# A decode-attention kernel rewritten with semaphores by hand: 8 heads per 8 MB tile, three slots, products in place

## The chip, the cores and the metric

The kernel runs on one core of a Trainium2 chip; the other cores are idle. The metric is device time in microseconds (us), the median of several executions. A profiled execution shows a span about 2 us shorter than its timed one; the span runs from the first to the last instruction.

## The reference, cut to what matters

One token for each of four sequences goes through a layer norm, attention over a cache of 4096 keys and values with 32 heads of 128, and a small MLP.

```python
B, Sq, D = 4, 1, 640
H, Sk, Dh, F = 32, 4096, 128, 1728
q = (layernorm(x) @ wq)                        # wq: 640 x 4096
scores = einsum("bhqd,bhkd->bhqk", q, k_cache) * Dh**-0.5
o = einsum("bhqk,bhkd->bhqd", softmax(scores), v_cache)
h = x + o @ wo                                 # wo: 4096 x 640
a = layernorm(h) @ w1 + b1                     # w1: 640 x 1728
out = h + (a * tanh(softplus(a))) @ w2         # w2: 1728 x 640
```

The two caches are bf16 and hold 134 MB each. With the weights, 283.3 MB have to be read once. Each byte of K is used in one multiply and one add, so this is a kernel that moves data.

## The kernel before

K and V come in tiles of 4 heads of one sequence, 4 MB each, into four rotating slots. All loads are issued from one queue (SP), each as soon as its slot is free. VectorE (DVE) multiplies a quarter of K by the broadcast query into a `prod` buffer; TensorE (PE) folds the 128 products of a key to 16 by eight matmuls against an identity; DVE sums these 16; ScalarE (ACT) takes the exponential. PE then multiplies the weights `e` with V.

```python
def emit_mult(i, s):
    t = work.tile([P, RS, Dh], BF16, tag="prod", name="prod", bufs=2)
    nc.vector.tensor_tensor(out=t, in0=kt[i][:, s*RS:(s+1)*RS, :], in1=q_bc[...], op=ALU.mult)
def emit_fold(i, s):
    for c in range(Dh // CW):
        nc.tensor.matmul(red, lhsT=ident, rhs=t[:, :, c*CW:(c+1)*CW], start=(c == 0), stop=...)
# ... (cut)
# order of the last loads:
loads.append((load_cache, vt, A_v_cache, NT - 1, "v", 4))   # the last V, in quarters
loads.append((load_wo_late,))                               # the second half of wo
for k in reversed(range(WLATE)):                            # the first half of wo, earlier
    loads.insert(2 * ((k + 1) * N - 1), (load_wo, k))
loads.append((load_mlp,))                                   # w1 in three loads, w2 in three
```

After the last V the rest has to be done in order: O, its product with `wo`, a layer norm, `w1`, the activation, `w2`, the stores. This stretch is called the tail below.

The softmax here doesn't subtract the row's maximum and nothing guards it: scores larger than these inputs give would overflow.

## Time and profile before

| | before |
|---|---|
| time, median (three executions; 669.59 with a fourth, in the result below) | 669.33 us |
| span of the profiled run | 667.5 us |
| bytes read | 283.4 MB |
| PE / DVE busy | 64% / 62% |
| DMA, 60 to 630 us | 432 GB/s, busy share 1.00 |

The page's totals by engine:

```profile
span 667.5 us, 6967 instructions
PE 426.0 (64%) x2937; PEld 198.2 (30%) x2937; DVE 411.7 (62%) x477; ACT 75.5 (11%) x312; POOL 1.9 (0%) x9
```

The windows view of the same run, for the start, the long middle and the end. Each row gives the stretch, its length, the busy time of each engine with its instructions, then the granted PE clock, the busy share of the DMA engines, and the GB/s moved. A DMA packet (one row of a load) counts in the stretch in which it starts:

```profile
core 0: us, PE busy (x) PEld busy (x) DVE busy (x) ACT busy (x) POOL busy (x), PEclk, DMA share, GB/s
0.00:60.00 60.00, 34.76 (x182) 14.52 (x183) 34.68 (x62) 11.79 (x30) 1.94 (x9) 0.95 0.98 411
60.00:630.00 570.00, 362.19 (x2390) 164.65 (x2389) 363.39 (x384) 57.97 (x267) 0.00 (x0) 0.83 1.00 432
630.00:667.50 37.50, 29.02 (x367) 19.05 (x365) 13.62 (x33) 5.76 (x15) 0.00 (x0) 0.68 0.81 337
```

The middle decides how to think about this kernel. No compute engine is near full, but the DMA share is 1.00 for 570 us.

The timeline view of the tail (start, duration, engine, line, operation; in brackets the idle time before it and what ended it):

```profile
646.49 0.61 PE L352 MATMUL pv_124<-v_3666,e 128*16 128x512 bf16 x8 [1.04 <-DMA v_3666<-in_A_v_cache_dram]
...
652.66 0.69 PE L409 MATMUL y_ps<-a_3986,wo_late 128*128 128x4 bf16 x20 [0.86 <-DMA wo_late<-in_A_wo_dram]
...
656.90 1.89 PE L537 MATMUL h_ps<-cen,w_slot 128*64 128x4 bf16 x28 [0.20 <-DMA w_slot<-in_B_w_dram]
...
662.41 1.91 PE L585 MATMUL y_ps<-w_sb,act 128*4 128x160 bf16 x52
664.37 0.33 DVE L591 CAST o_bf<-y_ps 128x160 bf16<-128x160 f32 x1 [2.24 <-PE y_ps L585]
664.72 0.67 SPq L594 DMA_DIRECT2D out_dram<-o_bf  x2
```

PE starts on the last quarter of V at 646.5 us, on the last part of `wo` at 652.7, on the second load of `w1` at 656.9, each time after a wait for that load.

### The profile page before, as it was taken

Reading aid. Unit: us, or ns where it says so; the run is one execution under the profiler, and the core shown is the slowest. Engines: PE = TensorE matmul, PEld = TensorE weight load, DVE = VectorE, ACT = ScalarE, POOL = GpSimd, SP = SyncE. Lnnn points to the kernel's source line nnn. Section 1 sums busy time; section 2 is a strip of 40 time slices with the busy share of each in tenths; the row PEclk is TensorE's granted clock in tenths of the full one; section 3 lists DMA queues with packets and bytes.
Section 4 is the critical chain, followed back from the end, with each engine's and each line's share of the span. In section 5 each row is a group of like instructions: output and inputs, shape, how many; then the busy total and the mean of one; then the engine's idle time right before and its main releaser. Section 6 shows DMA issues by size and latency. Waiting matters only on the chain.

```text
span 667.5 us, 6967 instructions
## 1 busy us (share of the span) xinstructions
PE 426.0 (64%) x2937; PEld 198.2 (30%) x2937; DVE 411.7 (62%) x477; ACT 75.5 (11%) x312; POOL 1.9 (0%) x9
## 2 busy tenths in 40 slices
PE   1967546694567675574764865568765657747586
PEld 0323222242223332232332422233322223323145
DVE  3387565686565676465675666557765657757542
ACT  0401001010001110011100110101100111001011
POOL 1000000000000000000000000000000000000000
PEclk9987789897788976788877788979867898778895
DMA  9999999999999999999999999999999999999995
GB/s 376 440 411 438 419 438 435 432 427 439 432 427 430 430 436 429 438 437 423 432 437 431 433 428 436 437 430 427 434 437 436 429 429 432 438 431 430 427 415 241
DMA packets 12591, 283.81 MB, mean 425 GB/s; under 512 B 1608, under 2 KB 1680, under 8 KB 3728
## 3 DMA queue, kind: packets, MB, share of 16 engines
q1 hardware_dynamic: 12224, 283.27, 98.8%
q8 instruction: 23, 0.38, 0.2%
q10 hardware_dynamic: 336, 0.10, 0.1%
q14 instruction: 8, 0.07, 0.0%
HBM read 283.36 MB, written 0.01 MB: 424 GB/s over the span
## 4 chain that ended last, share of the span: by engine, by line
DMA 61%; DVE 19%; PE 18%; issue 1%; ACT 0%; SPq 0%; DVEq 0%; ACTq 0%
DVE prod L284 16%; PE red L296 14%; DMA k_1005<-in_A_k_cache_dram 4%; DMA k_530<-in_A_k_cache_dram 4%; DMA k_1480<-in_A_k_cache_dram 4%; DMA k_1955<-in_A_k_cache_dram 4%; DMA k_2881<-in_A_k_cache_dram 4%; DMA k_2428<-in_A_k_cache_dram 4%; DMA k_3334<-in_A_k_cache_dram 4%; DMA k_1691<-in_A_k_cache_dram 4%; DMA k_310<-in_A_k_cache_dram 4%; DMA k_3092<-in_A_k_cache_dram 4%; DMA k_1216<-in_A_k_cache_dram 3%; DMA k_741<-in_A_k_cache_dram 3%; DMA v_3666<-in_A_v_cache_dram 3%; DMA k_2166<-in_A_k_cache_dram 3%
## 5 line engine op out<-in xcount | busy, mean ns | idle before, releaser
L296 PE MATMUL red<-prod,ident 128*128 128x512 bf16 x1024 | 300.1, 451 | 218.9 <-DVE prod L284 218.0
L296 PEld LDWEIGHTS <-ident 128*128 128x128 bf16 x1024 | 116.0, 114 | 385.2 <-issue 317.6
L313 DVE TENSOR_REDUCE s_f<-red 128x32 f32<-128x512 f32 x128 | 88.1, 688 | 79.4 <-PE red L296 79.2
L316 ACT ACTIVATE ex<-s_f 128x32 bf16<-128x32 f32 x128 | 29.3, 229 | 516.6 <-DVE s_f L313 516.6
L323 DVE TENSOR_TENSOR e<-ex,hmask 128x128 bf16<-128x128 bf16 x128 | 36.5, 285 | 6.1 <-ACT ex L316 6.1
L373 PEld LDWEIGHTS o_ps<-selo,pv_sb 128*128 128x128 f32 x256 | 34.0, 194 | 6.0 <-ACT pv_sb L363 1.2
L352 PEld LDWEIGHTS <-e 128*16 128x16 bf16 x1024 | 22.6, 89 | 36.8 <-issue 15.5
L373 PE MATMUL o_ps<-selo,pv_sb 128*128 128x4 f32 x256 | 31.1, 245 | 0.7 <-ACT pv_sb L363 0.7
L316 ACT ACTIVATION_READ_ACCUMULATOR ex<-s_f 128x1 f32 x128 | 23.9, 187 | 0.1
L284 DVE TENSOR_TENSOR prod<-k_79,qbc 128x4096 bf16<-128x4096 bf16 x4 | 9.1, 2287 | 17.6 <-DMA k_79<-in_A_k_cache_dram 17.6
L379 DVE TENSOR_TENSOR OT<-o_ps,rl 128x16 bf16<-128x16 f32 x8 | 1.6, 195 | 21.0 <-PE o_ps L373 21.0
L256 PE MATMUL q_ps<-wq_74,lnT 128*4 128x512 bf16 x32 | 10.7, 470 | 4.7 <-DMA wq_74<-in_A_wq_dram 4.7
L284 DVE TENSOR_TENSOR prod<-k_1691,qbc 128x4096 bf16<-128x4096 bf16 x4 | 9.1, 2286 | 5.7 <-DMA k_1691<-in_A_k_cache_dram 5.7
L284 DVE TENSOR_TENSOR prod<-k_3092,qbc 128x4096 bf16<-128x4096 bf16 x4 | 9.1, 2286 | 5.7 <-DMA k_3092<-in_A_k_cache_dram 5.7
L284 DVE TENSOR_TENSOR prod<-k_1216,qbc 128x4096 bf16<-128x4096 bf16 x4 | 9.1, 2286 | 4.9 <-DMA k_1216<-in_A_k_cache_dram 4.9
L284 DVE TENSOR_TENSOR prod<-k_3545,qbc 128x4096 bf16<-128x4096 bf16 x4 | 9.1, 2286 | 4.9 <-DMA k_3545<-in_A_k_cache_dram 4.9
L284 DVE TENSOR_TENSOR prod<-k_741,qbc 128x4096 bf16<-128x4096 bf16 x4 | 9.1, 2285 | 4.9 <-DMA k_741<-in_A_k_cache_dram 4.9
L284 DVE TENSOR_TENSOR prod<-k_903,qbc 128x4096 bf16<-128x4096 bf16 x4 | 9.1, 2287 | 4.8 <-DMA k_903<-in_A_k_cache_dram 4.8
L284 DVE TENSOR_TENSOR prod<-k_428,qbc 128x4096 bf16<-128x4096 bf16 x4 | 9.1, 2286 | 4.6 <-DMA k_428<-in_A_k_cache_dram 4.6
L284 DVE TENSOR_TENSOR prod<-k_1378,qbc 128x4096 bf16<-128x4096 bf16 x4 | 9.1, 2286 | 4.5 <-DMA k_1378<-in_A_k_cache_dram 4.5
L284 DVE TENSOR_TENSOR prod<-k_1853,qbc 128x4096 bf16<-128x4096 bf16 x4 | 9.1, 2286 | 4.5 <-DMA k_1853<-in_A_k_cache_dram 4.5
L284 DVE TENSOR_TENSOR prod<-k_530,qbc 128x4096 bf16<-128x4096 bf16 x4 | 9.1, 2285 | 4.4 <-DMA k_530<-in_A_k_cache_dram 4.4
(179 smaller groups left out, 376.2 us busy)
## 6 DMA issues: line engine op xcount, KB each, us to landing
wq_74<-in_A_wq_dram SPq DMA_DIRECT2D x1, 4096.0 KB
k_79<-in_A_k_cache_dram SPq DMA_DIRECT2D x1, 4096.0 KB, 24.8
k_81<-in_A_k_cache_dram SPq DMA_DIRECT2D x1, 4096.0 KB, 33.9
v_83<-in_A_v_cache_dram SPq DMA_DIRECT2D x1, 4096.0 KB, 17.3
k_244<-in_A_k_cache_dram SPq DMA_DIRECT2D x1, 4096.0 KB
v_246<-in_A_v_cache_dram SPq DMA_DIRECT2D x1, 4096.0 KB
k_310<-in_A_k_cache_dram SPq DMA_DIRECT2D x1, 4096.0 KB, 24.6
v_314<-in_A_v_cache_dram SPq DMA_DIRECT2D x1, 4096.0 KB, 32.1
```

Of the source, the lines that this page charges most:

```text
L256: nc.tensor.matmul(q_ps[:, :], lhsT=lnT[:, c, :], rhs=wq_t[c // WQC][:, o : o + 512], start=(c == 0), stop=(c == DC - 1),)
L284: nc.vector.tensor_tensor(out=t[:, :, :], in0=kt[i][:, s * RS : (s + 1) * RS, :], in1=q_bc[hg][:, b, :].unsqueeze(1).to_broadcast([P, RS, ...
L296: nc.tensor.matmul(red[:, :, :], lhsT=ident[:, :], rhs=t[:, :, c * CW : (c + 1) * CW], start=(c == 0), stop=(c == Dh // CW - 1),)
L313: nc.vector.tensor_reduce(out=s_t[i][:, sl], in_=reds.pop((i, s))[:, :, :], axis=AX.X, op=ALU.add)
L316: nc.scalar.activation(out=ex_t[i][:, sl], in_=s_t[i][:, sl], func=ACT.Exp, scale=SCALE, accum_out=rs_t[hg][:, b, s : s + 1],)
L323: nc.vector.tensor_tensor(out=e_t[i][:, sl, :], in0=ex_t[i][:, sl].unsqueeze(2).to_broadcast([P, RS, G]), in1=hmask[:, :].unsqueeze(1).to_ ...
L352: nc.tensor.matmul(pvs[i % 2][k * QD : k * QD + RQ * G, :], lhsT=e_t[i][:, u * RQ : (u + 1) * RQ, :], rhs=vt[i][:, u * RQ : (u + 1) * RQ, ...
L373: nc.tensor.matmul(o_ps[hg][:, b, :], lhsT=t[:, r, :], rhs=selo[:, r, :], start=(r == 0), stop=(r == RQ - 1),)
L379: nc.vector.tensor_tensor(out=OT[:, hg * G : (hg + 1) * G, :].rearrange("p g b -> p b g"), in0=o_ps.pop(hg)[:, :, :], in1=rl.pop(hg)[:, :] ...
```

## The change

The intent: fewer and larger loads, fewer instructions, no scheduling layer. The main parts are these.

- Tiles of 8 heads, 8 MB per load, in three slots of 64 KB per partition. The product overwrites K in its slot.
- 960 of the 1024 fold matmuls reuse the identity already in PE and have no weight load. PE's program is a loop.
- O is accumulated with one row per head and batch (`selo` as weights) instead of one column.
- With three such slots the program has about 16 KB per partition of SBUF left for all the rest (bytes 16512 to 32736 in its code), and `wo` needs 40 KB, so all of `wo` is loaded after the last V. The last V is one load.
- Every engine's program is written in order, with waits on counted semaphores.

```diff
-    G = 4
+    G = 8
-    NSLOT = 4
+    # three slots A, B, C of R * Dh elements
+    KS = {0: "A", 1: "B", 2: "A", 3: "B"}
+    VS = {0: "C", 1: "C", 2: "A", 3: "C"}
 # loads, one group of four tiles
+            k_load(i)                     # after PV of tile i-2
+            k_load(i + 1)                 # after the last fold of i-1
+            v_load(i)                     # after PV of i-1
+            k_load(i + 2)                 # after the last fold of i
+            v_load(i + 1)                 # after PV of i
+            k_load(i + 3)                 # after the last fold of i+1
+            v_load(i + 2)                 # after the last fold of i+2
+            v_load(i + 3)                 # after PV of i+1
 # ... and after the last tile: wo in 4 loads, w1 in 2, w2's remainder, w2 in 3
 # products in place
+                lambda: v.tensor_tensor(
+                    out=t, in0=t, in1=q_bc[:, hg, b, :].unsqueeze(1).to_broadcast([P, RS, Dh]),
 # one weight load per 16 fold matmuls
+            mm(*args, skip=False) if first else mm_same(*args)
 # O in row form
+                o_ps, selo[:, r, BG - G - b * G : 2 * BG - G - b * G], pv_sb[:, r, :],
 # ... (most of the diff is cut)
```

## The prediction

> **What bounds the kernel now.** The DMA stream. The windows view gives DMA share 1.00 and 432 GB/s over 60:630 us (431 to 433 in each 100 us). PE is busy 64%, DVE 62% (page). The chain of waits is 61% DMA; its DVE and PE pieces are work done while the next loads are queued. [...]283.3 MB at 432 GB/s is 656 us of the 667.5 us span. The rest: the first 10 us at 351 GB/s (about 2 us lost), and 10.6 us from the last w1 chunk's landing (656.9) to the end. Rearranging PE or DVE work can gain little[...].
>
> **What the change does.**
> - Same bytes. K/V come in 32 loads of 8 MB (64 KB rows) instead of 64 of 4 MB: perhaps less overhead; my estimate is 0 to 3 us.
> - PE: 1024 fold matmuls stay, 960 of their weight loads go (451 ns mean each now). 1024 PV matmuls stay (1.90 us per 32). Off the critical path.
> - DVE: same elements, half the instructions. Per 8 MB tile, estimated from 2.29 us per 4096 columns and 0.69 us per 512 reduced: 18 + 5 + 2.5 = 25.5 us, against 38.8 us of loads. Still hidden.
> - Slots: three of 8 MB, products in place, so K is held until its last fold. Landings lag the average byte count by about 5 us. At 19.4 us per load I find every slot free before its turn; the smallest slack is V of a group's third tile (waits for the fold after PV), about 6 us[...]. Few small bubbles: 0 to 4 us.
> - Start: all of q comes before the first product, so DVE starts some 10 us later, but the first V needs its slot only at 52 us: hidden.
> - Tail: worse. All of wo (5.2 MB, 160 matmuls, weights now strided) comes after the last V; before, half was done earlier. The last V lands whole, not in quarters. After it I estimate, from the trace: PV 3.9, copy and O 2, sums, `om` and transposes 3, wo 160 matmuls at 33 to 67 ns partly waiting for loads, layer norm 1.3, w1 70 at 67 ns 4.7, activation and 40 small matmuls 2.5 to 4, w2 2.2, output 3.5: 29 to 33 us. Before, 21 us from the last V quarter (646.5) to the end. The last V lands about 6 us earlier (2.6 MB more behind it). Net +2 to +6 us.
>
> **Sum.** Steady state -3 to +4, tail +2 to +6, start 0, lighter synchronisation perhaps -1 to -3. A hand-made schedule was probably tuned, so I lean low: 668 us timed, 659 to 677. Chances: faster by over 2% 0.06, within 2% 0.87, slower 0.07.
>
> **What would show each step.** Windows: 60:630 at 431 to 435 GB/s, DMA share 0.99 or more, no 10 us window under 0.9. Queue's waits: K/V issues wait for PV or fold, yet no gap. Groups: [...]960 fewer PEld, PE busy down by 40 us or more with no time gained. Timeline at the end: last V landing near 640, 27 to 33 us from there to the end, PE waiting little on DMA.
>
> **What would make it wrong.** If 8 MB loads with 64 KB row pitch run at another rate (1% is 6.5 us either way); if a slot frees late in each group, bubbles of several us times four; if PE's loop or self-loading weights cost more; if the tail overlaps better than my serial sum.

## The result

| | before | after |
|---|---|---|
| time, median | 669.59 us | 669.56 us |
| PE busy / weight loads busy | 426.0 / 198.2 us | 394.1 / 79.4 us |
| DMA, 60 to 630 us | 432 GB/s | 433 GB/s |
| PE starts on the last of V | 646.5 us | 637.2 us |
| PE starts on the last part of `wo` | 652.7 us | 650.7 us |
| last byte of the weights moved | 662.6 us | 661.4 us |
| end of span | 667.5 us | 667.4 us |

The ratio after to before is 1.000, with a 95% interval of 0.9985 to 1.0014. Ratios here are the mean time of one kernel's runs over that of the other's of the same rounds, so not quite the ratio of the medians quoted. The time of the last byte comes from the trace's packet records: each weight load has its own row size, so its packets can be told apart.

The page and the windows view of the changed kernel:

```profile
span 667.4 us, 5166 instructions
PE 394.1 (59%) x2729; PEld 79.4 (12%) x1769; DVE 406.5 (61%) x250; ACT 41.0 (6%) x157; POOL 2.6 (0%) x14
```

```profile
0.00:60.00 60.00, 32.11 (x234) 13.19 (x183) 23.86 (x23) 7.38 (x15) 2.02 (x11) 0.77 0.99 419
60.00:630.00 570.00, 339.02 (x2081) 47.45 (x1170) 377.43 (x205) 29.96 (x138) 0.61 (x3) 0.80 1.00 433
630.00:667.40 37.40, 22.97 (x416) 18.77 (x416) 5.18 (x22) 3.70 (x5) 0.00 (x0) 0.60 0.76 311
```

A quarter of the instructions and 119 us of weight loads are gone, and the middle looks the same, since the DMA share was 1.00 and still is. The tail in the timeline of the changed kernel:

```profile
637.21 5.27 PE L657 MATMUL pv<-slotC,e 128*32 128x512 bf16 x64 [11.19 <-PEq L44]
...
642.41 1.76 PE L657 MATMUL y_ps<-a_t,slotB 128*128 128x4 bf16 x40
...
650.66 1.73 PE L657 MATMUL y_ps<-a_t,slotB 128*128 128x4 bf16 x40 [1.15 <-PEq L44]
...
654.00 2.73 PE L657 MATMUL red<-cen,slotB 128*64 128x4 bf16 x42 [0.30 <-PEq L44]
...
661.44 1.96 PE L657 MATMUL red<-slotA,act 128*4 128x160 bf16 x52
663.44 0.32 DVE L653 CAST o_bf<-red 128x160 bf16<-128x160 f32 x1 [2.53 <-PE red L657]
663.79 1.33 SPq L239 DMA_DIRECT2D out_dram<-o_bf  x4
```

In this hand-synchronised program the profile names PE's own sequencer (PEq) as what ended a wait, at L44, the `wait_ge` of the program's helper; what it waited for has to be worked out from the program. The 11.19 us are the wait for the last V, the 1.15 us the wait for the last quarter of `wo`.

At the last V the changed kernel is 9.3 us ahead. About 6.2 us of that is only order, by an estimate at 433 GB/s: 2.7 MB more (half of `wo` and the remainder of w2) now lie behind V. Some 3 us are a real lead. At the last part of `wo` the lead is 2.0 us, at the last byte 1.2, at the end 0.1. So a gain was there and was given back in the last 30 us. The windows show the GB/s of one place, 650 to 655 us, first before, then after, then for the loads of the changed kernel without any compute (stream8, below):

```profile
650.00:655.00 5.00, 3.59 (x82) 3.16 (x78) 0.97 (x7) 1.38 (x2) 0.00 (x0) 0.50 1.03 423
```

```profile
650.00:655.00 5.00, 3.77 (x60) 3.62 (x61) 1.54 (x11) 0.83 (x2) 0.00 (x0) 0.50 1.03 385
```

```profile
650.00:655.00 5.00, 0.00 (x0) 0.00 (x0) 1.00 1.01 377
```

The third line warns against a hasty reading: 385 is lower than 423, but the same loads move no more when nothing runs beside them. (The windows of runs without compute have columns for DVE and POOL alone.)

The theory going into the experiments was: the stream of bytes bounds the middle, and at the end the last byte and the chain of work after the last V arrive together. The rivals were: a gain of PE or DVE that late slots eat up; 8 MB loads that run at another rate; and an end set by the chain after the last V alone.

### The profile page after: what moved, and what is told of

It reads as the page before. It is cut to its first block, busy times and chain, and to the rows that moved or that the text cites. A ratio compares the mean times of both kernels' runs of the same rounds, so it can differ in the third digit from the quotient of the medians.

```text
span 667.4 us, 5166 instructions
## 1 busy us (share of the span) xinstructions
PE 394.1 (59%) x2729; PEld 79.4 (12%) x1769; DVE 406.5 (61%) x250; ACT 41.0 (6%) x157; POOL 2.6 (0%) x14
## 5 line engine op out<-in xcount | busy, mean ns | idle before, releaser
L466 DVE TENSOR_TENSOR slotA<-slotA,q_bc 128x8192 bf16<-128x8192 bf16 x32 | 140.7, 4416 | 110.9 <-DMA slotA<-in_A_k_cache_dram 110.7
L466 DVE TENSOR_TENSOR slotB<-slotB,q_bc 128x8192 bf16<-128x8192 bf16 x32 | 140.7, 4416 | 16.3 <-DMA slotB<-in_A_k_cache_dram 16.3
L667 PE MATMUL red<-slotA,ident 128*128 128x512 bf16 x480 | 141.0, 459 | 0.0
L477 DVE TENSOR_REDUCE s_f<-red 128x64 f32<-128x1024 f32 x64 | 78.1, 1220 | 96.9 <-PE red L667 96.8
L667 PE MATMUL red<-slotB,ident 128*128 128x512 bf16 x480 | 123.3, 415 | 0.0
L657 PE MATMUL red<-slotA,ident 128*128 128x512 bf16 x32 | 14.2, 445 | 119.3 <-PEq L44 119.3
L657 PE MATMUL pv<-slotC,e 128*32 128x512 bf16 x768 | 52.4, 434 | 42.7 <-PEq L44 42.7
L657 PE MATMUL red<-slotB,ident 128*128 128x512 bf16 x32 | 14.1, 441 | 87.0 <-PEq L44 87.0
L348 ACT ACTIVATE ex<-s_f 128x64 bf16<-128x64 f32 x64 | 16.4, 256 | 502.3 <-DVE s_f L477 502.3
L491 DVE TENSOR_TENSOR e<-ex,hmask 128x512 bf16<-128x512 bf16 x64 | 39.8, 682 | 0.0
L657 PEld LDWEIGHTS pv<-slotC,e 128*32 128x32 bf16 x768 | 22.5, 108 | 103.0 <-issue 89.4
L657 PE MATMUL o_ps<-pv_sb,selo 128*32 128x128 f32 x128 | 17.0, 276 | 0.0
## 6 DMA issues: line engine op xcount, KB each, us to landing
slotA<-in_B_w_dram SPq DMA_DIRECT2D x1, 320.0 KB, 30.2
```

Of the source, the lines that this page charges most:

```text
L348: lambda: a.activation(out=ex[:, sl], in_=s_f[:, sl], func=ACT.Exp, scale=SCALE, accum_out=rs[:, b, s : s + 1],),
L466: lambda: v.tensor_tensor(out=t, in0=t, in1=q_bc[:, hg, b, :].unsqueeze(1).to_broadcast([P, RS, Dh]), op=ALU.mult,),
L477: lambda: v.tensor_reduce(out=s_f[:, s * RS : (s + 1) * RS], in_=red[:, k : k + 2, :].rearrange("p k (r c) -> p (k r) c", c=CW), axis=AX.X ...
L491: lambda: v.tensor_tensor(out=e[:, sl, :], in0=ex[:, sl].unsqueeze(2).to_broadcast([P, RS, G]), in1=hmask[:, :].unsqueeze(1).to_broadcast( ...
L657: lambda: nc.tensor.matmul(out_, lhsT=lhsT, rhs=rhs, start=start, stop=stop, skip_group_check=skip),
L667: return t.add_instruction(mybir.InstMatmult(name=nc.get_next_instruction_name(), engine=mybir.EngineType.PE, ins=[t.lower_ap(rhs), t.lowe ...
```

## The experiments

### The loads alone, 8 MB and 4 MB

Compute is removed; each load waits for the landing of the one before it in its slot.

```diff
 # stream8: loads and order of the changed kernel
-            sp.need(("F", i, NS - 1))     # and all waits for PV and folds
+            sp.need(held[s])              # the slot's previous load has landed
 # stream4: loads, sizes and order of the kernel before, in the same frame
```

> The changed kernel's loads alone (8 MB, three slots, each load waiting only for the landing of the one before it in its slot); no compute, wrong result on purpose. Theory 'the byte stream is the bound': the 60:630 us stretch still moves 432 to 434 GB/s, the last bytes move at 659 to 662 us (changed kernel 661.4), and the time is 665 to 668 us, shorter than the changed kernel only by the w2 matmuls and the cast that follow the last bytes there. Rival 'late slots cost bubbles in the changed kernel': last bytes by 656 us or earlier and a time of 662 us or less.

> The kernel before's loads alone (4 MB, four slots), no compute, wrong result on purpose. 'The byte stream is the bound, whatever the size of a load': within 2 us of stream8, and 431 to 433 GB/s over 60:630. Rival '8 MB loads with 64 KB rows run at another rate': over 4 us from stream8.

Measured: 664.81 us for 8 MB loads and 667.67 us for 4 MB, beside 669.35 us of the kernel before on that chip. The middle of each, first 8 MB, then 4 MB:

```profile
60.00:630.00 570.00, 0.00 (x0) 0.00 (x0) 1.00 1.00 434
```

```profile
60.00:630.00 570.00, 0.00 (x0) 0.00 (x0) 1.00 1.00 431
```

(In this stretch the 4 MB stream also moved half of `wo`, in 5 KB rows.) The 8 MB stream is 2.9 us shorter. That is less than the 4 us that the rival named and more than the 2 us of my theory; the direction is settled, and it agrees with the 3 us of lead at the last V. In these two streams a 64 KB row took 2.421 us on one DMA engine and a 32 KB row 1.216 us (medians of the packet records; 2.421 and 1.213 in the two kernels), so one large row is 11 ns faster than two small ones: 433.1 against 431.2 GB/s over 16 engines. For the 4096 large rows on 16 engines that makes 2.8 us, an estimate, and so nearly all of the 2.9. The number of loads was halved as well, and no run separates the two.

The bare 8 MB stream moved its last byte at 658.8 us, just below my range of 659 to 662, and its time was just below 665. The late-slot rival, with 656 us and 662 us, is further off. But the theory's "only by the w2 matmuls and the cast" was too simple: in the changed kernel the last byte comes 2.6 us later than in the bare stream. About 1.2 us of it are there when the last 64 KB row ends (636.6 against 635.4 us), the rest arises in the weight loads. In the kernel before the last byte is 0.9 us later than in its own bare stream. So the new kernel starts from a stream 2.9 us shorter, and sits 4.7 us above it where the old one sat 1.7 us above its own.

### Weight loads restored

```diff
-            mm(*args, skip=False) if first else mm_same(*args)
+            mm(*args, skip=False)
```

> The changed kernel with a weight load ahead of every fold matmul again (960 more). 'The byte stream is the bound': PE's weight-load busy time rises by 80 us or more, PE busy by some 10 to 30 us, the time stays 669 to 671 us. Rival 'the gain of shared weights is real and was lost elsewhere': 673 us or more.

Measured: 670.08 us, ratio 1.001 (0.9993 to 1.0026) to the kernel before. The page's totals:

```profile
PE 394.9 (59%) x2729; PEld 181.7 (27%) x2729; DVE 406.4 (61%) x250; ACT 41.0 (6%) x157; POOL 2.6 (0%) x14
```

Weight loads rose by 102 us and PE busy by 0.8 us. My 10 to 30 us of PE time were wrong: the shared weights saved PE next to nothing. (The 451 ns that the prediction gives beside these loads is the mean of a fold matmul's record; the weight load's own record has 114 ns.) Eight fold matmuls with their weight loads took 1.89 us before, which is a step of about 216 ns; fifteen without take 3.40 us, again about 216 ns (one matmul's 0.38 us taken off, divided by 7 and by 14; both at a granted clock of 1.00). So the weight loads ran beside the matmuls. The 32 us that PE lost came from elsewhere, above all from O in row form (31.1 us of matmuls before, 17.0 after) and the packed q projection (14.2 us before, 3.8 after).

### How near are the three slots to being late?

```diff
+            for n in range(2):
+                dv.do(<the same mask multiply into e>, ("x", i, s, n), "DV")
+                dv.need(("x", i, s, n))
```

> The changed kernel with every mask multiply done three times (about 5.3 us more of DVE per tile, 85 us in all, DVE then busy some 490 of 667 us): how near are its slots to being late? My reading of its queue: the tightest load is V of a group's third tile, issued 26.8 us before it lands while it takes 19.4 us to move, so about 7 us of slack. Two earlier tiles' masks and its own delay that fold by some 8 to 11 us, so I expect a hole of 0 to 5 us in each of four groups: 669 to 690 us, best guess 680. 'DVE's share of the span is what counts' expects 669 to 671, since DVE stays well under 100%.

Measured: 696.95 us, from 692 to 699, ratio 1.042 (1.039 to 1.044). DVE is busy 494.5 of 690.5 us in the profile, 72%, and still the stream has holes. The queue's issues of the third tile's V, in the timeline of SP, changed kernel first, slower one second:

```profile
280.69 0.33 SPq L239 DMA_DIRECT2D slotA<-in_A_v_cache_dram  x1
```

```profile
291.74 0.33 SPq L239 DMA_DIRECT2D slotA<-in_A_v_cache_dram  x1
```

And the DMA in the windows view of the slower one at that place:

```profile
286.00:294.00 8.00, 6.70 (x64) 1.74 (x41) 3.64 (x5) 1.28 (x5) 0.00 (x0) 1.00 0.57 205
288.00:290.00 2.00, 2.00 (x13) 0.10 (x1) 0.00 (x0) 0.58 (x1) 0.00 (x0) 1.00 0.00 0
290.00:292.00 2.00, 2.00 (x12) 0.37 (x5) 0.26 (x1) 0.00 (x0) 0.00 (x0) 1.00 0.00 0
```

No row starts between 287.5 and 292.7 us. The rows already under way run until 290.2, so the time in which nothing moves at all is 2.5 us. The packet records show four such holes, at 131, 288, 448 and 609 us, with 2.0, 5.2, 6.2 and 5.2 us from one row's start to the next: at V of the third tile in each of the four groups, where I had put the smallest slack. The size was above my range (up to 690 us), and the holes are not all of it. In the profiled run (692.3 us) the last row of V ends 16.8 us later than in the changed kernel (653.4 against 636.6), but PE then waits until 660.6 for DVE, which is not done with the last masks; that the tail too would be late was left out of the expectation. So the rewrite has about 7 us of slack at that place, seen also from its issue to its landing in the unchanged version:

```profile
slotA<-in_A_v_cache_dram SPq DMA_DIRECT2D x4, 26.8
```

The load takes 19.4 us (8.39 MB at 433 GB/s), so it stands in the queue 7.4 us before its turn. That is enough for the kernel as it is: in its packet records no two row starts between 20 and 635 us are more than 1.6 us apart. The late-slot rival falls.

### Cutting the tail: the last V in quarters, w2 not loaded, and both

```diff
 # vq: the last V in four loads, PV starts on each
+            if i == NT - 1 and u % (nu // VQ) == 0:
+                pe.need(("V", i, u // (nu // VQ)))
 # now2: w2 is set by GpSimd instead of loaded (wrong result on purpose)
+            po.do(lambda: g.memset(w2_sb[:, j0:j1, :], 0.001), ("w2", j0), "PO")
```

> The changed kernel with the last V load in four quarters and PV starting on each as it lands: takes about 4 us off the chain that follows the last V (PV 5.3 us then). 'Two limits end together' (chain and last bytes both at about 661 us): saves only 1 to 2 us, 667.5 to 668.6 us, and the w2 matmuls then wait for the last w2 load. Rival 'the chain after the last V alone sets the end': saves 3.5 to 4.5 us, 665 to 666 us. Rival 'the bytes alone set it': saves under 0.7 us.

> The changed kernel with 2.1 MB fewer bytes at the very end (w2 is set by GpSimd, not loaded; wrong result on purpose): the last bytes move about 5 us earlier. 'Two limits end together': saves under 1 us, because the chain after the last V still ends at about 661 us: 668.6 to 669.6. Rival 'the bytes alone set the end': saves about 5 us, 664 to 665.

> Both edits. 'Two limits end together': now both limits have moved, so it saves more than the sum of the two alone, 3.5 to 5 us: 664.5 to 666. If either limit alone set the end, it would be equal to that edit alone.

Measured: 669.67, 669.27 and 669.34 us, beside 669.38 us of the kernel before. All three are the same within noise. The first two could be read as two limits that coincide, but the third speaks against that: with both moved, nothing was gained either. The theory of these two limits fell.

The timeline of the version in quarters shows PV finished early, and what came after:

```profile
637.73 1.90 PE L664 MATMUL pv<-slotC,e 128*32 128x512 bf16 x16 [3.02 <-PEq L44]
...
640.96 1.73 PE L664 MATMUL y_ps<-a_t,slotB 128*128 128x4 bf16 x40 [1.34 <-PEq L44]
...
644.53 0.40 PE L664 MATMUL y_ps<-a_t,slotB 128*128 128x4 bf16 x6
...
647.09 1.52 PE L664 MATMUL y_ps<-a_t,slotB 128*128 128x4 bf16 x34 [2.15 <-issue]
...
654.24 2.77 PE L664 MATMUL red<-cen,slotB 128*64 128x4 bf16 x42 [0.30 <-PEq L44]
```

PE is done with PV at 639.6 us instead of 642.5, waits for `wo`, and then stands for 2.15 us in the middle of 40 equal matmuls, with "issue" as the reason: nothing that the profile shows. The `w1` matmuls start at 654.24 us, as before the edit (654.00). The version with both edits has the same gap of 2.15 us, so its result alone would not tell a gap from a third limit. Two things were noted: PE's gap, and that `wo` and `w1` have landings of their own.

### w1 ahead of wo

```diff
-            load(<wo, 4 loads>)
-            load(<w1, 2 loads>)
+            load(<w1, 2 loads>)
+            load(<wo, 4 loads>)
```

> The changed kernel with its two w1 loads (2.2 MB, about 5.2 us of stream) moved ahead of the four wo loads; same bytes, same last byte, last V lands as before. New theory after the quarters gave nothing: the end is set by the landing of wo's last quarter (650.6 us in the changed kernel) plus the 16.8 us of work that follows it. It expects wo's last quarter at about 655.7 and the time up by 4 to 5 us: 673.5 to 675. Rivals 'last V plus its chain' and 'last byte' both expect 669 to 670.

Measured: 675.04 us, ratio 1.008 (1.007 to 1.010). The tail in its timeline:

```profile
637.41 5.43 PE L657 MATMUL pv<-slotC,e 128*32 128x512 bf16 x64 [11.19 <-PEq L44]
...
656.11 1.73 PE L657 MATMUL y_ps<-a_t,slotB 128*128 128x4 bf16 x40 [2.27 <-PEq L44]
...
669.18 1.33 SPq L239 DMA_DIRECT2D out_dram<-o_bf  x4
```

The last V lands as before and the last byte moves at 660.7 us, even earlier than in the changed kernel. The only thing that moved later is the landing of `wo`, by 5.4 us, and the end moved by 5.4 us with it (span 672.8 against 667.4). From there to the end it is 16.7 and 16.8 us. So the place of `wo` in the stream is a limit of its own.

### The order of the tail alone, in the kernel before

```diff
-    loads.append((load_cache, vt, A_v_cache, NT - 1, "v", 4))
-    loads.append((load_wo_late,))
-    for k in reversed(range(WLATE)):
-        loads.insert(2 * ((k + 1) * N - 1), (load_wo, k))
+    loads.append((load_cache, vt, A_v_cache, NT - 1, "v"))
+    loads.append((load_wo_late, 0, WLATE))
+    loads.append((load_wo_late, WLATE, NWB))
```

> The kernel before with the change's tail order alone: all of wo after the last V, and the last V in one load. My prediction's step: all of wo behind the last V costs +2 to +6 us, so 671 to 675. 'wo's last part plus what follows, or the last byte, sets the end': the bytes behind wo's last part are the same as before (w1, w2), so under 1 us: 668.7 to 670.3.

Measured: 670.18 us against 669.45, ratio 1.0012 (0.9999 to 1.0026). All of `wo` behind the last V, and V in one load, cost 0.7 us, which is not clear of noise, and not 2 to 6 (the interval ends at 1.7 us). Even these 0.7 us may not be the order's, for PE has a gap like that of vq here:

```profile
654.21 0.33 PE L408 MATMUL y_ps<-a,wo_late 128*128 128x4 bf16 x7 [1.27 <-issue]
```

The bytes behind the last part of `wo`, `w1` and `w2`, are the same in both orders, and the last packet of `wo` ends at about the same time: 652.3 us in the kernel before, 652.0 here.

### Versions meant to beat both

vq_out2 has the quarters and sends two of the four stores from ACT's queue. best2 also loads the last quarter of `wo` in two pieces. best3 adds 76 useless matmuls where PE waits for the last V anyway.

```diff
+        out_loads(sp, 0)     # stores 0 and 2 from SP
+        out_loads(ac, 1)     # stores 1 and 3 from ACT
 # best2
+                load(sp, wo_sb[:, q, G - 2 : G, :], wv[:, G - 2 : G, :], ("wo", q, 1), "W9")
 # best3, ahead of the last tile's PV
+            for _ in range(76):
+                mm(misc[:, 256:384], ident[:, :], ident[:, :], True, True)
```

> A version meant to beat both kernels: quarters of the last V, and the four output stores issued from two queues (two each) instead of four in a row on one (1.33 us of issues). Expect vq less 0.4 to 0.8 us: 666.8 to 668.0.

> The version with the last V in quarters and output stores from two queues, plus wo's last quarter cut in two loads (30 of its 40 matmuls run before the last piece lands). Takes about 1 us off the chain behind wo's landing; the last w2 load (lands about 662.1, used at about 663.0) allows some 0.9 us. Expect 667.6 to 668.6, 0.1 to 0.3% below both kernels.

> The last version (quarters, two store queues, wo's last quarter in two pieces) with 76 matmuls of no use (into an unused part of PSUM) put on TensorE before the last tile's PV, where it waits for V anyway. Theory: in that version PE stands still for 2.15 us in the wo matmuls with nothing to wait for, while a 16 KB packet of the instruction queue is moved (644.7 to 645.8 us in the quarters run)[...]. It expects no such gap after 640 us, and 667.0 to 668.3 us, 0.6 to 1.9 less than without. If the gap is not a refill, or a refill stalls as long elsewhere: 668.6 to 669.2.

A "refill" here is such a packet, taken as PE's next instructions. The 76 matmuls (152 instructions with their weight loads) were put there to move it away from the gap's place. That its place depends on the number of PE instructions ahead was the assumption; no run shows it.

Measured, each against the kernel before of its rounds: vq_out2 668.89 us (before 669.38; ratio 0.9991, 0.9977 to 1.0005), best2 668.89 us (669.45; 0.9991, 0.9977 to 1.0004), best3 669.09 us (669.41; 0.9995, 0.9982 to 1.0009). None is clear of noise against the kernel before, and each missed the range that its theory expected (best3 lies in that of its rival). Against vq in the same rounds the second store queue gained 0.8 us (668.89 against 669.67). By the traces, the issuing is 0.7 us of that: four issues took 1.34 us on one queue (vq), two took 0.66 us on each of two (vq_out2).

Cutting `wo`'s last quarter gained nothing, and neither did closing PE's gap. In best3 that gap is gone, and another wait has taken its place:

```profile
644.31 1.76 PE L671 MATMUL y_ps<-a_t,slotB 128*128 128x4 bf16 x40
...
650.25 1.73 PE L671 MATMUL y_ps<-a_t,slotB 128*128 128x4 bf16 x40 [0.59 <-PEq L44]
...
654.32 2.71 PE L671 MATMUL red<-cen,slotB 128*64 128x4 bf16 x42 [1.03 <-DVE b1s L618]
```

No gap with "issue" as its reason is left; PE waits 0.59 us for the last quarter of `wo`, and then the w1 matmuls wait 1.03 us. The profile names `b1s`, the event that ended last by its own account, but these matmuls do not need it. The last packet of the first `w1` load ends at 653.5 us in this run, and in another run that waits there (vq_out2, below) the matmuls start 0.65 us after that packet (653.4, 654.0), as here after 0.8. So PE waits for that load to land, an inference from the packet records.

```profile
654.02 2.77 PE L669 MATMUL red<-cen,slotB 128*64 128x4 bf16 x42 [0.67 <-PEq L44]
```

In the changed kernel itself that packet ends at 653.1 us, so by the same delays the load could be used from 653.8 or 653.9 on (an estimate), and the w1 matmuls start at 654.0. By this estimate they could have started hardly any earlier, however early `wo` was done. In the changed kernel and the six versions of its tail with `wo` first they start between 654.00 and 654.36 us.

The gap itself fits a refill of PE's instructions. The instruction queue moved 23 packets of 16 KB in the kernel before and 10 in the changed kernel, and none in stream8, where PE has nothing to do. In vq one was moved from 644.7 to 645.8 us, at the start of the gap, and PE went on 1.27 us after the packet's end. In the four other runs with such a gap (now2_vq, vq_out2, best2, before_late) it is 1.2 to 1.3 us as well. With 152 more PE instructions ahead (best3), no gap is there, though a packet was moved from 644.4 to 645.5 us: a packet alone does not stop PE. If the gap is a wait for that packet, it took 2.15 us in vq, beside a DMA share of 0.96 (644.9 to 647.1 us). That the missing packet caused the gap is argued from time and place; no run took the refill away.

## Why the prediction was right, and where it was not

The time was 669.56 us for a predicted 668, well inside 659 to 677, and "within 2%" was the outcome given 0.87.

- **"What bounds the kernel now: the DMA stream."** Right. The middle stayed at a DMA share of 1.00, at 433 GB/s; the same loads without compute (stream8) moved 434 there.
- **"Perhaps less overhead; my estimate is 0 to 3 us."** Right, at its upper edge: 2.9 us between the two bare streams.
- **"PE, off the critical path."** Right, and ldw shows it with the shared weights alone. The size was wrong: "PE busy down by 40 us or more" was 32 us, and ldw puts 0.8 us of it down to the weight loads.
- **"The smallest slack is V of a group's third tile, about 6 us."** Right in place (mask3) and nearly in size (7.4 us). "Few small bubbles" was pessimistic: the packet records show none.
- **"Start: hidden."** Right. The first product starts 10 us later (26.5 against 36.4 us), the first V load is issued at 31.7 us, and 20:60 moves as in the bare stream (426 and 423 GB/s).
- **"Tail: 29 to 33 us from the last V."** It took 30.2 us, with little waiting on DMA in it (1.15 us, for `wo`), as predicted.
- **"Net +2 to +6 us" from the tail.** The size came out and the reason did not. From the last V to the end it is 30.2 us instead of 21.0; less the 6.2 us that are only order, the tail costs 3.0 us, and the faster stream ("Steady state -3 to +4") pays for them. But the prediction's reason was the order: all of `wo` behind the last V, and V whole. In the kernel before that order costs 0.7 us, within noise, and PV done 2.9 us earlier (vq) saved nothing. The prediction added up the work after the last V as if that were the only way into the tail. There are four, and each load lands about when its work can start. That the sum fits all the same is partly luck.
- **"668 us timed."** The middle of the prediction's own ranges would be about 672 us; 668 came from leaning low. That a gain and a loss of 3 us cancel to within 0.1 us is luck too.
- **"Lighter synchronisation perhaps -1 to -3."** No sign of it, and no run tests it alone. As the stream is the bound, there was little for it to shorten.

The four ways in, in the changed kernel:

| what lands | first use | from there to the end | which run moved it | effect |
|---|---|---|---|---|
| last V | 637.2 us | 30.2 us, with 1.15 us of waiting in it | vq | none |
| last quarter of wo | 650.7 us | 16.8 us | w1first, later by 5.4 us | +5.4 us of span |
| first load of w1 | 654.0 us | 13.4 us | seen as the wait in best3 | next limit |
| last byte of w2, 661.4 us | about 663 us | about 4.4 us | now2 | none |

The third column is the end of the span less the first use; the last row is an estimate from the place of the last load's matmuls among the 52. Taking the wait for `wo` away uncovered the next one, for the first load of `w1` (best3), which in the changed kernel lies only 0.1 to 0.2 us behind, by the estimate above. Edges this close together explain why edits to the tail gave nothing one by one, and two of them nothing together. That moving all of them would give a gain is argued, not shown.

Where did the expected gain go? Of the 2.9 us that larger loads are worth, the changed kernel still had about 3 at the last V. At the last part of `wo` the lead is 2.0 us, and from there to the end the changed kernel needs 1.9 us more (16.8 against 14.9). About 1.0 of that is the 40 matmuls that wait for its last part instead of 20 (1.77 us against 0.73 until DVE copies the sum), and about 0.8 is the stretch from the last cast to the end (4.0 us against 3.2), where four stores on one queue are 0.7. The versions that took both on (best2, best3) came out 0.6 and 0.3 us below the kernel before, within noise; in best3 the first load of `w1` is the next limit.

The other microsecond was lost while the weights were loaded: the 9.7 MB after the last 64 KB row took 24.8 us (636.6 to 661.4), against 23.4 us in its bare stream (635.4 to 658.8). The rows themselves took no longer: those of the weights add up to 23.8 us if 16 engines share them evenly, against 23.6. They are spread wider. The first row of the last w2 load starts 0.6 us later than in the bare stream (657.3 against 656.7), its last row ends 2.6 us later. The program waits for whole loads, so the spread costs what a lower rate would. The trace does not tell which DMA engine a packet was on, so what falls behind, and why it does so beside compute, was not settled. And the version that combines all edits with a finer first `w1` load was not run.

## What to carry to other kernels

When a DMA share is 1.00 for most of the span, price a rewrite by what it does to the stream: here larger loads gave 2.9 us, and 119 us less of weight loads gave nothing. A kernel tuned to its stream can have a tail where every landing is just in time, as here, so ask of each load how much serial work lies behind it, and be ready to have to move several of these edges before any gain shows. A bare stream (the loads without the compute) is a cheap run that tells how much there is at most left to win with these loads in this order: 4.7 us of 669.6 here.
